# A fused attention and two-layer chain: q turned in 32x32 blocks, tokens in natural order, a new start list

## The chip, the cores and the metric

One NeuronCore of one Trainium2 chip runs the whole program. The metric is the time of one execution on the device in microseconds (us), the median of several runs; lower is better. The engines are TensorE (PE in the profile; PEld are its weight loads), VectorE (DVE), ScalarE (ACT), GpSimd (POOL) and SyncE (SP), whose queue issues most DMAs.

## The reference

Inputs: q, k, v of shape (8 batches, 8 heads, 576 tokens, 64), phi of shape (8, 8, 576, 32), and four weight matrices of doubles: 512x2048 and 2048x512 for each of two layers. Cut to what matters:

```python
a = softmax(phi, axis=2 (tokens))           # per batch, head and memory slot
k_m = einsum('bhsm,bhsd->bhmd', a, k)       # 32 memory slots a head
v_m = einsum('bhsm,bhsd->bhmd', a, v)
attn = softmax(q @ k_m^T / 8, axis=-1)      # over the 32 slots
x = (attn @ v_m) as (8*576 tokens, 512)     # heads side by side
x = square(relu(x @ w_in)) @ w_out          # first layer
h = x @ w2_in
out = (h - tanh(h)) @ w2_out                # second layer
```

## The kernel before, in words

The work has two layers in time. In the first, tokens go in 16 units of 288 (two for a batch); a unit takes 16 steps, one for each 128 of the 2048 hidden channels. In the second, tokens go in nine blocks of 512, again 16 steps each. Every large matmul is split into a high and a low part (hi*hi, hi*lo, lo*hi), so a step of the first layer is six matmuls into h (L425) and twelve into four accumulators (L454 to L456), all with 288 columns. The kernel doesn't form attn @ v_m: `u_make` multiplies v_m of a batch into 512 columns of w_in (u, L285), and h is u times the attention weights.

`att_a(b, g)` handles four heads (g = 0 or 1) of batch b. It loads phi, k and v with tokens in six chunks of 96, takes the maximum of phi over tokens (L216, a transpose on TensorE L221, a second maximum L223, a broadcast matmul L229), subtracts and exponentiates (L232, L236), sums over chunks on GpSimd (L239 to L241), multiplies with v and k (L246, 6 chunks x 4 heads; L248 for the sum), scales (L255), transposes (L261) and copies into `vt` and `kt`.

`att_b(b, o)` handles the four even or the four odd heads. It loads q in chunks of 96 tokens, transposes it on TensorE (L320, twelve a call) and copies it by ScalarE (L325, L326), multiplies with kt (scores, L334, eight matmuls of 64 rows by 32 columns), turns the scores in 32x32 blocks on VectorE (L343), makes the softmax with VectorE, GpSimd and ScalarE (L347 to L357), turns back (L360), and writes the hi (L364, ScalarE) and lo part (L366, GpSimd) of the attention weights. Tokens of a batch are dealt to the chunks in turn, p*6 + c, and the two units of a batch each hold tokens of all chunks by that order; a unit needs both calls of `att_b`.

The weights come as 64-bit doubles and are converted by `conv`: the absolute value on ScalarE (L144), then four VectorE instructions (L146 clamp, L148 shift and mask, L149 sign, L150 low bits). The 16 tiles of w_in go to `w1_conv`, the 16 of w_out to `wo_conv`, which splits them on GpSimd (L186). The second layer's 32 tiles are converted during the first layer and stored to DRAM (`w2_conv`).

The order of instructions is written by a manual schedule. Each piece of work is a generator; at each `yield` it names the buffers that it wants next, and it goes on only when they are free. For the first two batches and a part of the third, the text `ORDER` lists which generator is advanced next (i: att_a, j: att_b, w and o: conversions, u: u_make, S: a step of the first layer); what can't go on is tried again later. `step(s)` issues the h matmuls three steps ahead of the accumulating ones. The other batches start at fixed steps (`at_step`): for batch b, with s = 32(b-1) - 20, att_a at s and s + 8, att_b at s + 10 and s + 17. Engines run their instructions in order, so a waiting instruction holds up those behind it on its engine.

The output is stored by 70 DMAs on SyncE's queue and two on ScalarE's (L609), in pieces that follow the dealt order of tokens.

Of the kernel before, what the change touches and what calls it, by code (L numbers as in the profile page):

```python
# [9 lines left out]
F32 = mybir.dt.float32  # L10
# [11 lines left out]
P = 128  # L22
SP = 96
NC = 6
HT = 288
FT = DFF // P
# [14 lines left out]
w00 w00 o11 w02 i01 o0 w11 i00 u01 o2 w10 o8 w22 o12 j00 i00 i01 w02 w01 w02 i00 o0 i21 i00 i00 o3 j11 o0 w00 i00 w03  # L41
w20 w02 i00 w02 w00 o3 w10 i00 w01 w01 o0 w03 w03 w12 w10 i00 i01 j01 w02 j00 o1 o2 i00 o0 j00 i01 w00 w02 j01 j01 i20
w00 w13 i00 i00 i00 o12 w00 w03 o0 o4 w31 o1 i01 i10 i01 o4 w23 o0 j00 o9 j01 i01 w03 o1 j01 i01 j01 w01 w10 j01 o2
i01 w01 u00 o4 o15 i01 o2 i01 u01 o12 o2 i01 w03 w21 i01 i01 w03 o1 w01 j01 j01 o4 w13 o13 o0 j01 o4 o1 j20 w11 w00
u00 u00 j01 j01 w11 j01 o2 o4 w21 i00 o6 u00 o2 o12 w11 w21 o1 o3 w12 o4 o1 o4 j01 j00 j00 j01 o1 j00 w30 j00 w31 j00
w21 o12 o7 j01 i10 j01 i10 i10 o2 i10 w11 j00 i10 i11 o12 j01 o3 o2 j00 i10 o12 i10 w10 j11 w31 w31 i11 o0 w02 j00 o12
w12 i10 w03 i11 j00 j00 o5 o4 o5 o3 w13 o3 i10 j00 j00 o14 S i10 o10 i11 w12 i11 w13 o5 i10 j00 j11 S i11 w00 w12 i11
w01 S S o3 i11 w20 w11 o3 i11 i10 o5 i01 i20 j11 o10 o3 S i11 S j11 w13 w10 w11 o7 i10 o7 w13 o7 w32 w00 w32 o6 j11
w33 o8 i11 i11 o7 i11 u10 S u12 j11 j11 j11 o6 j10 S o7 o5 o7 o5 w10 j11 j11 o6 j10 w12 S u01 o5 j10 u01 o5 j11 w12
u10 i20 o7 u01 o10 o6 j10 o6 j10 o8 j11 S u11 o7 o6 u10 o10 j11 w23 j01 j11 w21 j21 o6 w23 o10 j10 o1 j10 u12 j11 j11  # L50
j10 S j10 j20 o2 w23 S o8 j10 o10 w23 o8 o12 j10 w21 j10 w01 j10 S o8 w22 j10 j10 w22 S S o11 w20 w22 w21 w23 j10 j10
S w21 j20 u11 S i20 w21 u11 o8 w22 w02 o11 S j20 S w20 S j20 w31 o11 o10 o1 o10 w22 w22 j20 o9 o14 o11 w11 S o11 w31
# [12 lines left out]
i20 w32 j21 j21 S j21 j20 w21 w33 S j21 S i20 j20 w11 i20 j21 j21 j21 j21
# [3 lines left out]
W_LO = 2.0 ** -15  # L69
W_HI = float.fromhex("0x1.dffffep+16")  # L70
# [3 lines left out]
def moe_chain_kernel(ctx: ExitStack, tc: tile.TileContext, q, k, v, phi, w1i, w1o, w2i, w2o, out):  # L74
    nc = tc.nc
    w1i, w1o, w2i, w2o = (w.bitcast(I32) for w in (w1i, w1o, w2i, w2o))
    out_v = out.rearrange("(b p c) e -> b c p e", b=B, c=NC)
# [7 lines left out]
    p_s9 = pool("small9", 1)  # L85
    pool("pad0", 1).tile([P, 8], F32, name="pad0")
# [17 lines left out]
    a_kv = pool("a_kv", 4, att)  # L104
# [3 lines left out]
    a_kt = pool("a_kt", 2, att)  # L108
    a_one = pool("a_one", 1, att)
# [23 lines left out]
    def conv(src, out, p=None, ahead=1):  # L133
# [14 lines left out]
        nc.vector.tensor_scalar(fi, fi, 3, 0x3FFFFFF8, op0=ALU.logical_shift_left, op1=ALU.bitwise_and)  # L148
        stt(fi, raw[:, :, 1], -0x40000000, fi, op0=ALU.bitwise_and, op1=ALU.bitwise_or)  # L149
# [9 lines left out]
    def w1_conv(fc, pr, p=None):  # L159
        if pr == 0:  # L160
            yield "w1"
            w1[0, fc] = slot(p_w, [P, 4, 512], f"w1_{fc}")
        while (0, fc) not in w1:
# [6 lines left out]
        done.add(("stored", fc, pr))  # L170

    def w1_load(b, fc):
        while not {("stored", fc, pr) for pr in range(4)} | {("u", 1, c) for c in range(FC)} <= done:
            yield
# [25 lines left out]
    def att_a(b, g, p_kv):  # L200
        yield "ph kv" if p_kv is a_kv else "ph"
        ph = slot(a_in, [SP, 4, NC, M], f"phi{b}_{g}")
        heads = slice(4 * g, 4 * g + 4)
        nc.sync.dma_start(ph, phi[b, heads].rearrange("h (p c) m -> p h c m", c=NC))
        yield "" if p_kv is a_kv else "wo wo wo wo"
        kv = []
        for h in range(4 * g, 4 * g + 4):
            t = slot(p_kv, [SP, 2, NC, D], f"kv{b}_{h}")
            for i, src in enumerate((v, k)):
                nc.sync.dma_start(t[:, i], src[b, h].rearrange("(p c) d -> p c d", c=NC))  # L210
            kv.append(t)
        for _ in range(4 if b > 2 else 1):
            yield
        yield "e f"
        m1 = slot(p_f, [SP, P], "m1")
        nc.vector.tensor_reduce(m1, ph.rearrange("p h c m -> p h m c"), axis=AX.X, op=ALU.max)  # L216
        yield "b"
        mx = p_s.tile([P, 1], F32, tag="mx", name="mx")
        den = p_s.tile([P, 1], F32, tag="den", name="den")
        t = psum(ps_b, "m1T")  # L220
        nc.tensor.transpose(t[:, :SP], m1, ident[:SP, :SP])  # L221
        yield "-"
        nc.vector.reduce_max(mx, t[:, :SP], axis=AX.X)  # L223
        dg = slot(p_f, [P, P], "dg")
        nc.scalar.activation(dg, ident, AF.Copy, scale=mx)
        give("b")
        yield "b"
        t = psum(ps_b, "mb")
        nc.tensor.matmul(t[:SP, :P], ones, dg)  # L229
        yield "-"  # L230
        e = slot(a_e, [SP, NC, 4, M], f"e{b}_{g}")
# [45 lines left out]
    def u_make(b, fc):  # L277
# [16 lines left out]
        if b:  # L294
            give("w1")
# [474 lines left out]
```

## Time and profile before

| what | value |
|---|---|
| median of 3 runs | 1581.09 us (1577.79 to 1581.84) |
| span of the profiled execution, first to last instruction | 1578.4 us |
| the median less that span | 2.7 us |
| busy share PE, PEld, DVE, ACT, POOL | 97%, 84%, 66%, 55%, 38% |
| data moved | 163 MB, 103 GB/s over the span |

The profile is of one execution, and durations are its own; the profiled execution's own time is the span and the small part around it, for which the table's third row stands. PE is busy when any matmul is under way; matmuls overlap, so the sum of their durations is more than PE's busy time, and prices of small matmuls are read from start times. The idle time of an engine that is not the bottleneck costs nothing.

### The profile page before, as it was taken

The page shows a single profiled execution, that of the slowest core. Times are in us where ns is not written, and L with a number is a line of the kernel's source. Part 1 is how long each engine was busy: PE and PEld are TensorE (multiplying, and loading weights), DVE is VectorE, ACT ScalarE, POOL GpSimd, SP SyncE. Part 2 cuts the span into 40 slices and gives each one's busy share as a digit, 9 for nine tenths or more (in the row PEclk, how much of TensorE's full clock was granted, in tenths as well). Part 3 has the DMA queues.
Part 4 walks back from the last instruction along what each step waited for, and adds up shares of the span by engine and source line. Part 5 has one row for each costly group of instructions (what it writes and reads, how often), then busy time and mean ns, then how long its engine had stood idle before and what let it go on. Part 6 is the DMA issues. An engine that isn't in the chain of part 4 may idle for free.

```text
span 1578.4 us, 26135 instructions
## 1 busy us (share of the span) xinstructions
PE 1523.9 (97%) x9904; PEld 1329.9 (84%) x9904; DVE 1043.0 (66%) x1436; ACT 868.1 (55%) x1849; POOL 605.2 (38%) x578
## 2 busy tenths in 40 slices
PE   4688999999999999999999999999999999999998
PEld 2577999999999999999988888888888888888887
DVE  5878444454535545430088888888889888888886
ACT  3576677666667676665554444444444444444433
POOL 2556465443534443443334232333324242333321
PEclk9999999999999999999999999999999999999999
DMA  9447566563745555431480101010010101010000
GB/s 329 152 139 175 185 154 171 175 213 111 239 138 196 181 174 173 137 123 69 150 308 1 42 12 43 11 31 24 1 41 14 42 13 43 12 44 11 25 3 27
DMA packets 89854, 163.06 MB, mean 103 GB/s; under 512 B 12416, under 2 KB 65664, under 8 KB 86656
## 3 DMA queue, kind: packets, MB, share of 16 engines
q1 hardware_dynamic: 86080, 157.52, 31.4%
q0 software_dynamic: 3456, 3.54, 1.7%
q8 instruction: 78, 1.28, 0.3%
q14 instruction: 48, 0.39, 0.1%
q10 hardware_dynamic: 192, 0.33, 0.1%
HBM read 117.96 MB, written 43.38 MB: 102 GB/s over the span
## 4 chain that ended last, share of the span: by engine, by line
PE 91%; DVE 3%; DMA 3%; ACT 2%; issue 1%; POOL 1%; SPq 0%; ACTq 0%; POOLq 0%
PE h L545 25%; PE h L425 13%; PE o L591 8%; PE o L590 8%; PE o L589 8%; PE acc L456 8%; PE acc L455 8%; PE acc L454 8%; PE u L285 2%; PE vkm L246 1%; PE qT L320 1%; DMA w_d<-w 1%; PE sc L334 1%; DVE wf L150 1%; DMA raw<-in_moe_w_in 1%
## 5 line engine op out<-in xcount | busy, mean ns | idle before, releaser
L545 PE MATMUL h<-x,wi 128*128 128x512 f32 x1728 | 414.7, 389 | 0.0
L575 POOL TENSOR_TENSOR gl<-pl,gh 128x512 fp32r<-128x512 f32 x144 | 187.9, 1305 | 535.7 <-PE o L590 517.2
L545 PEld LDWEIGHTS h<-x,wi 128*128 128x128 f32 x1728 | 324.2, 188 | 67.5 <-POOL x L525 0.2
L442 POOL TENSOR_TENSOR g<-gg,g 128x288 fp32r<-128x288 f32 x256 | 226.1, 902 | 366.2 <-ACT g L441 284.3
L557 ACT ACTIVATE u<-h 128x512 f32<-128x512 f32 x144 | 86.1, 598 | 418.3 <-PE h L545 418.3
L456 PE MATMUL acc<-g,wo 128*128 128x288 f32 x1024 | 301.8, 295 | 0.0
L454 PE MATMUL acc<-g,wo 128*128 128x288 f32 x1024 | 301.5, 294 | 0.2 <-ACT xs L465 0.2
L455 PE MATMUL acc<-g,wo 128*128 128x288 f32 x1024 | 301.3, 294 | 0.0
L425 PE MATMUL h<-aT,u 128*128 128x288 f32 x1536 | 259.3, 304 | 5.0 <-ACT gg L437 3.9
L425 PEld LDWEIGHTS h<-aT,u 128*128 128x128 f32 x1536 | 217.2, 190 | 39.3 <-issue 20.0
L589 PE MATMUL o<-wo,gh 128*128 128x512 f32 x576 | 224.1, 389 | 0.0
L590 PE MATMUL o<-wo,gh 128*128 128x512 f32 x576 | 224.1, 389 | 0.0
L591 PE MATMUL o<-wo,gl 128*128 128x512 f32 x576 | 224.1, 389 | 0.0
L454 PEld LDWEIGHTS acc<-g,wo 128*128 128x128 f32 x1024 | 192.8, 188 | 0.5 <-ACT xs L465 0.4
L455 PEld LDWEIGHTS acc<-g,wo 128*128 128x128 f32 x1024 | 192.6, 188 | 0.0
L456 PEld LDWEIGHTS acc<-g,wo 128*128 128x128 f32 x1024 | 192.6, 188 | 0.0
L560 DVE SCALAR_TENSOR_TENSOR pl<-u 128x512 f32<-128x512 f32 x144 | 99.5, 691 | 94.7 <-ACT u L557 94.7
L437 ACT ACTIVATE gg<-h 128x288 f32<-128x288 f32 x256 | 104.8, 409 | 88.8 <-PE h L425 86.3
L564 DVE SCALAR_TENSOR_TENSOR pl<-pl,u 128x512 f32<-128x512 f32 x144 | 148.6, 1032 | 0.0
L565 DVE COPY_PREDICATED pl<-m,th 128x512 f32<-128x512 int32 x144 | 140.2, 974 | 4.9
L590 PEld LDWEIGHTS o<-wo,gh 128*128 128x128 f32 x576 | 108.1, 188 | 22.6
L591 PEld LDWEIGHTS o<-wo,gl 128*128 128x128 f32 x576 | 108.1, 188 | 22.3
(86 smaller groups left out, 1977.2 us busy)
## 6 DMA issues: line engine op xcount, KB each, us to landing
w<-w_d SPq DMA_DIRECT2D x24, 1024.0 KB, 6.2
raw<-in_moe_w_in SPq DMA_DIRECT2D x32, 512.0 KB, 4.5
raw<-in_moe_w_out SPq DMA_DIRECT2D x32, 512.0 KB, 5.5
w_d<-w2s SPq DMA_DIRECT2D x32, 512.0 KB, 3.1
kv<-in_v SPq DMA_DIRECT2D x64, 144.0 KB, 4.6
kv<-in_k SPq DMA_DIRECT2D x64, 144.0 KB, 4.5
q<-in_q SPq DMA_DIRECT2D x16, 576.0 KB, 5.7
x_d<-xs SPq DMA_DIRECT2D x64, 144.0 KB, 2.5
```

The source lines that it names most:

```text
L425: nc.tensor.matmul(t[:, :HT], uu[:, w, o, c], at[u // 2][:, x, o, u % 2 * HT:u % 2 * HT + HT], start=(n == 0), stop=(n == 5))
L442: nc.gpsimd.tensor_tensor(gl, gg, gh.bitcast(F32), op=ALU.subtract)
L454: nc.tensor.matmul(o, wh[:, c], gh, start=(f == a), stop=False)
L455: nc.tensor.matmul(o, wh[:, c], gl, start=False, stop=False)
L456: nc.tensor.matmul(o, wl[:, c], gh, start=False, stop=(f == z - 1))
L545: nc.tensor.matmul(t, wi[f][:, w, c, :], x, start=(n == 0), stop=(n == 11))
L564: stt(pl, pl, A0, u, op0=ALU.add, op1=ALU.mult)
L565: nc.vector.copy_predicated(pl, m.bitcast(I32), th)
L575: nc.gpsimd.tensor_tensor(lo, pl, hi.bitcast(F32), op=ALU.subtract)
L589: nc.tensor.matmul(o, gh[:, c], wh, start=(f == 0), stop=False)
L590: nc.tensor.matmul(o, gh[:, c], wl, start=False, stop=False)
L591: nc.tensor.matmul(o, gl[:, c], wh, start=False, stop=(f == FT - 1))
```

## The change

- `att_b` now handles a half of the tokens (r = 0 or 1) with all eight heads, and a unit needs only its own half. q of a batch is loaded once. For batches 1 to 7 it comes as 32x32 blocks (four DMAs, 32 partitions each, runs of 32 numbers), and VectorE's block transpose makes qt; the transposes on TensorE and the copies by ScalarE stay only for batch 0.
- Heads are grouped by four (g) in `kt`, the scores and `u`; a table `POS` says in which 32 columns each head lies.
- Tokens are in natural order. `att_a` has chunks of 128 tokens, four full ones and one of 64 whose rest is filled (phi with -3e38, k and v with 0). From batch 2 on k and v carry a column of ones, so that the sums come from the same matmul. Batch 0's second group has buffers and PSUM banks of its own.
- `conv` scales by a power of two on ScalarE and has three VectorE instructions.
- Waits on other generators are written as functions, so that the list doesn't advance a generator that can't go on.
- `ORDER` is new (598 entries, before 779). The first S is entry 86, before 204.
- Two output blocks of 128 tokens are stored by one DMA.

```diff
-NC = 6
+NC = 5
+NR = S - P * (NC - 1)
+NEG = -3.0e38
+TB = HT // 32
+POS = (0, 2, 1, 3, 2, 0, 3, 1)
...
+i00 i01 j00 w02 j01 i01 w00 i00 i01 i01 i01 i01 i01 w01 w02 i01 i00 i00 i00 i00 o2 i01 i01 w02 i01 w00 i01 w00 w00
+j00 w01 i00 w13 w01 w03 w03 w03 o0 o7 u11 i00 i00 o1 i00 i01 o1 i00 i00 i00 i01 i01 j00 o2 o3 j00 w00 o0 j01 j01 j00
+i00 w10 w02 j01 w02 j01 j01 i00 w12 w10 o0 w10 w00 j00 u00 j00 j00 j00 w02 j00 u00 w01 w11 w00 w00 S j01 w11 w03 j00
...
-        nc.scalar.activation(f, raw.bitcast(F32)[:, :, 1], AF.Abs)
-        yield
-        nc.vector.tensor_scalar(f, f, W_HI, W_LO, op0=ALU.min, op1=ALU.max)
+        nc.scalar.activation(f, raw.bitcast(F32)[:, :, 1], AF.Copy, scale=W_SCALE)
+        yield
         fi = f.bitcast(I32)
...
+        for x, src in zip(kv, (v, k)):
+            if dense:
+                nc.sync.dma_start(x[:, :, :NC - 1], src[b, heads, :n0].rearrange("h (p c) d -> p h c d", p=P))
+            else:
+                for h in range(4):
+                    nc.sync.dma_start(x[:, h, :NC - 1, :D], src[b, 4 * g + h, :n0].rearrange("(p c) d -> p c d", p=P))
+        for x, src in zip(kv, (v, k)):
+            nc.sync.dma_start(x[:NR, :, NC - 1, :D], src[b, heads, n0:].rearrange("h p d -> p h d"))
...
-        for c in range(NC):
-            for h in range(4):
-                nc.tensor.matmul(vkm[32 * h:32 * h + 32, :2 * D], e[:, c, h], kv[h][:, :, c, :],
-                                 start=(c == 0), stop=(c == NC - 1))
-        nc.tensor.matmul(vkm[:, 2 * D:2 * D + 1], s1[:, 0], ones[:SP, :1])
+        wd = D if dense else D + 1
+        for i in range(2 if own else 1):
+            for c in range(NC):
+                for h in range(4):
+                    x = kv[i][:, h, c] if own else (kv_d if dense else kv_s)[:, :, h, c]
+                    o = vkm[32 * h:32 * h + 32, i * D:(i + 1) * D] if own else vkm[32 * h:32 * h + 32, :2 * wd]
+                    nc.tensor.matmul(o, e[:, c, h], x, start=(c == 0), stop=(c == NC - 1))
+        if dense:
+            nc.tensor.matmul(vkm[:, 2 * D:2 * D + 1], s1[:, 0], ones[:, :1])
...
         for i in range(4):
-            for o in range(2):
-                nc.tensor.matmul(t[o][32 * i:32 * i + 32], vt[b][half(o), i], w[half(o), i])
+            for h in (i, i + 4):
+                r, p0 = half(h % 2), 32 * POS[h]
+                nc.tensor.matmul(t[h // 4][p0:p0 + 32], vt[b][r, h // 2], w[r, h // 2])
...
+            qs[b] = slot(a_q, [P, 4, 2 * TB, 32], f"q{b}")
+            for g in range(2):
+                for dh in range(2):
+                    src = q[b, 4 * g:4 * g + 4, :, 32 * dh:32 * dh + 32]
+                    p0 = 64 * g + 32 * dh
+                    nc.sync.dma_start(qs[b][p0:p0 + 32], src.rearrange("i (t p) d -> p i t d", p=32))
+            for _ in range(4 if b > 2 else 1):
+                yield
+        yield lambda: b in qs
         yield "qt"
         qt = slot(a_qt, [P, 4, HT], "qt")
...
+        if b:
+            nc.vector.transpose(qt.rearrange("p i (t n) -> p i t n", n=32), qs[b][:, :, r * TB:(r + 1) * TB])
...
         for i in range(4):
-            for r in range(2):
-                nc.tensor.matmul(t[r][32 * i:32 * i + 32, :HT], kt[b][half(r), 2 * i + o], qt[half(r), i, :])
+            for g in range(2):
+                p0 = 32 * POS[4 * g + i]
+                nc.tensor.matmul(t[g][p0:p0 + 32, :HT], kt[b][half(g), i], qt[half(g), i, :])
...
-            if (u // 2, f // 4) not in us or not {("b", u // 2, o) for o in range(2)} <= done:
+            if (u // 2, f // 4) not in us or ("b", u // 2, u % 2) not in done:
                 return False
...
+                if i % 2:
+                    q_out = nc.scalar if last else nc.sync
+                    q_out.dma_start(out[c0 - P:c0 + P, :].rearrange("(t p) e -> p t e", p=P), acc["t"])
```

## Rows read from the trace of the kernel before

**Rows 1.** The page: busy time by engine, and PE in 40 slices.

```profile
PE 1523.9 (97%) x9904; PEld 1329.9 (84%) x9904; DVE 1043.0 (66%) x1436; ACT 868.1 (55%) x1849; POOL 605.2 (38%) x578
...
PE   4688999999999999999999999999999999999998
```

**Rows 2.** Busy time by stretch: PE, PEld, DVE, ACT, POOL; granted clock, DMA share, GB/s.

```profile
0.00:63.10 63.10, 26.93 (x237) 16.96 (x238) 45.14 (x74) 24.19 (x48) 21.94 (x26) 1.00 0.78 253
63.10:160.00 96.90, 85.00 (x689) 74.91 (x688) 76.36 (x105) 68.97 (x165) 53.98 (x53) 0.98 0.61 164
160.00:1573.10 1413.10, 1411.93 (x8982) 1237.98 (x8981) 920.96 (x1258) 774.61 (x1637) 529.23 (x500) 1.00 0.30 92
1573.10:1578.40 5.30, 0.00 (x0) 0.00 (x0) 0.57 (x2) 0.37 (x1) 0.00 (x0) 0.83 0.58 179
```

**Rows 3.** PE's timeline, start-up: start, duration, line, count, idle time before and releaser.

```profile
12.22 3.13 PE L246 MATMUL vkm<-kv,e 96*32 96x128 f32 x48 [4.59 <-ACT e L236]
...
29.05 3.09 PE L246 MATMUL vkm<-kv,e 96*32 96x128 f32 x48 [0.48 <-DMA w_d<-w]
...
63.89 3.01 PE L425 MATMUL h<-aT,u 128*128 128x288 f32 x11 [0.20 <-POOL aT L366]
```

**Rows 4.** PE's timeline in the first layer, same columns.

```profile
300.68 0.29 PE L456 MATMUL acc<-g,wo 128*128 128x288 f32 x1
300.81 0.66 PE L320 MATMUL qT<-ident,q 96*128 96x96 f32 x6
...
302.13 0.29 PE L454 MATMUL acc<-g,wo 128*128 128x288 f32 x1
...
303.58 0.29 PE L456 MATMUL acc<-g,wo 128*128 128x288 f32 x1
...
304.50 0.29 PE L454 MATMUL acc<-g,wo 128*128 128x288 f32 x1
...
313.31 0.71 PE L334 MATMUL sc<-qt,kt 64*32 64x288 f32 x16
...
328.54 1.09 PE L285 MATMUL u<-w,vt 64*32 64x512 f32 x16
...
336.90 0.29 PE L456 MATMUL acc<-g,wo 128*128 128x288 f32 x1
337.12 1.52 PE L246 MATMUL vkm<-kv,e 96*32 96x128 f32 x48
338.56 0.38 PE L248 MATMUL vkm<-ones,s 96*128 96x1 f32 x2
338.81 1.05 PE L425 MATMUL h<-aT,u 128*128 128x288 f32 x6
339.70 0.29 PE L454 MATMUL acc<-g,wo 128*128 128x288 f32 x1
```

**Rows 5.** DVE's groups by line, 5 to 160 us: busy us, mean ns, idle before.

```profile
L146 DVE TENSOR_SCALAR w<-w 128x512 f32<-128x512 f32 x14 | 12.0, 855 | 6.3 <-ACT w L144 5.5 <-DMA w_d<-w 0.7
...
L146 DVE TENSOR_SCALAR wf<-wf 128x512 f32<-128x512 f32 x15 | 7.2, 482 | 5.3 <-ACT wf L144 5.3
...
L360 DVE STREAM_TRANSPOSE aT<-sm 128x576 f32<-128x576 f32 x4 | 3.1, 775 | 2.2 <-POOL sm L357 2.2
```

**Rows 6.** Busy time in one batch of the first layer (32 steps).

```profile
400.00:489.80 89.80, 89.80 (x808) 83.69 (x808) 44.36 (x66) 61.43 (x145) 39.61 (x44) 1.00 0.56 179
```

**Rows 7.** POOL's timeline: lo part of the first att_b.

```profile
49.69 1.74 POOL L366 TENSOR_TENSOR aT<-aT,aT 128x576 fp32r<-128x576 f32 x1 [1.72 <-ACT aT L364]
```

**Rows 8.** A stretch with one 16 KB load; q's issues: KB, us to landing.

```profile
1188.00:1188.40 0.40, 0.40 (x3) 0.34 (x2) 0.36 (x2) 0.40 (x1) 0.00 (x0) 1.00 0.27 40
...
q<-in_q SPq DMA_DIRECT2D x16, 576.0 KB, 5.7
```

**Rows 9.** DMA issues over the whole span: KB, us to landing.

```profile
w_d<-w2s SPq DMA_DIRECT2D x32, 512.0 KB, 3.1
...
out<-osb ACTq DMA_DIRECT2D x1, 128.0 KB, 2.8
```

More of the change, by code (lines that the diff above doesn't have):

```diff
@@ L170, in w1_conv, with w1_user @@
         done.add(("stored", fc, pr))
+        w1_user(fc)
+    w1_users = collections.Counter()
+    def w1_user(fc):
+        w1_users[fc] += 1
+        if w1_users[fc] == 5:
+            give("w1")
     def w1_load(b, fc):
-        while not {("stored", fc, pr) for pr in range(4)} | {("u", 1, c) for c in range(FC)} <= done:
-            yield
+        yield lambda: {("stored", fc, pr) for pr in range(4)} | {("u", 1, c) for c in range(FC)} <= done
         yield "w1"
@@ L328, in att_b @@
[L328 to L331 removed]
+        if b:
+            nc.vector.transpose(qt.rearrange("p i (t n) -> p i t n", n=32), qs[b][:, :, r * TB:(r + 1) * TB])
+            q_used[b] += 1
+            if q_used[b] == 2:
+                give("q")
+        else:
+            for n in range(2):
+                yield "" if early else "b b"
+                t = [psum(ps_a if early else ps_b, f"qT{i}") for i in range(2)]
+                for i in range(2):
+                    for c in range(3):
+                        nc.tensor.transpose(t[i][:, c * SP:(c + 1) * SP],
+                                            qs[b][n][:, i, 3 * r + c].rearrange("p g d -> p (g d)"), ident[:SP, :SP])
+                q_used[b] += 1
+                if q_used[b] == 4:
+                    give("u", "u")
+                yield "-"
+                for i in range(2):
+                    nc.scalar.copy(qt[:, 2 * n + i], t[i][:, :HT])
+                if not early:
+                    give("b", "b")
@@ L363, in att_b, with ready @@
             at[b] = slot(p_at, [P, 2, 2, 2 * HT], f"aT{b}", F32R)
-        nc.scalar.copy(at[b][:, 0, o], a)
+        hi, lo = (at[b][:, x, :, r * HT:(r + 1) * HT] for x in range(2))
+        nc.scalar.copy(hi, a)
         yield
-        nc.gpsimd.tensor_tensor(at[b][:, 1, o], a, at[b][:, 0, o].bitcast(F32), op=ALU.subtract)
-        give("sm")
-        done.add(("b", b, o))
+        nc.gpsimd.tensor_tensor(lo, a, hi.bitcast(F32), op=ALU.subtract)
+        if (b, r) != (0, 1):
+            give("sm")
+        done.add(("b", b, r))
     active, wants = [], {}
     emptied = []
+    def ready(gen):
+        want = wants.get(gen, "")
+        if callable(want):
+            return want()
+        need = collections.Counter(want.strip("-").split())
+        if any(free[r] < n for r, n in need.items()):
+            return False
+        free.subtract(need)
+        return True
     def empty():
@@ L418, in l1_mm1 @@
         u, f, _, _ = seq[s]
-        assert {("b", u // 2, o) for o in range(2)} <= done, u
+        assert ("b", u // 2, u % 2) in done, u
         uu, c = us[u // 2, f // 4], slice(f % 4 * P, f % 4 * P + P)
```

273 lines of the change are left out of this document (141 added, 132 removed).

## The prediction

> **What bounds the kernel now.** I read the page's slices first [rows 1]: TensorE (PE) is at 90% or more in 35 of 40 slices; only the first four and the last lie lower. Busy time is 1523.9 of 1578.4 us, so nothing but TensorE work or the idle 54.5 us can change the time. The table by stretch [rows 2] places that idle time: 36.2 us lie ahead of 63.1 us, where the first matmul of the first layer stands; 11.9 lie between there and 160 us, 1.2 in the next 1413 us, 5.3 behind the last matmul.
>
> So there are two regimes. From 160 us on an engine other than PE costs nothing, and each TensorE instruction removed comes off the end whole. Ahead of 160 us the start-up sets the pace: loads, 32 weight conversions, the attention of two batches. There the rows of the first matmuls [rows 3] show what the first layer waits for: the second group of heads multiplies 16.8 us after the first (29.05 against 12.22), and the first h matmul runs free at 63.89, just released by the lo half of aT, GpSimd's last step of the *second* half of the attention. VectorE is busy 76.4 of the 96.9 us that follow [rows 2].
>
> The sum stands against the profiled span of 1578.4 us; the median of the runs is 1581.1, so 2.7 us lie around the span, and I keep them. As worked in the terms below: 1578.4 = 63.1 (first h) + 1496.9 (TensorE work behind it, 1510.0 less 13.1 idle) + 13.1 + 5.3.
>
> **The change, part by part.**
>
> *q turned by VectorE.* Batches 1 to 7 lose all their transposes on TensorE: 24 each, in four groups of six. From the last L456 ahead of such a group to the first L454 behind the h matmuls is 302.13 - 300.68 = 1.45 us; in a step with no guest it is 304.50 - 303.58 = 0.92 [rows 4]. So 0.53 us a group, 2.12 a batch. ScalarE loses eight copies of qT, which hide behind PE. VectorE gains two block transposes a batch of 128x1152; the trace has one of 128x576 at 775 ns [rows 5], so 1.55 us by proportion; two of the half size would be the same, and nothing in the trace makes it less than 0.78. In a batch of 89.8 us VectorE is 44.4 us busy [rows 6], so 3 us more are covered; without that cover it would be 3 us a batch.
>
> *Token chunks of 128.* Each group of heads multiplies 20 times instead of 24. A group now costs 339.70 - 336.90 - 0.92 = 1.88 us, of which the 48 instructions of L246 take 338.56 - 337.12 = 1.44 and the pair of L248 338.81 - 338.56 = 0.25 [rows 4]. Five chunks instead of six, 130 columns instead of 128, make 1.22: 0.22 saved. From batch 2 on the column of ones in kv takes over L248's sum, another 0.25. So 0.94 us a batch for batches 2 to 7 and 0.44 for batch 1. GpSimd's three additions a group go too, under cover.
>
> TensorE in all: 6 x (2.12 + 0.94) + 2.12 + 0.44 = 20.9 us. Wholly behind PE's bound for batches 2 to 7 (18.4); for batch 1, in the ramp, I count it too, since it stands in the work term and not in the idle one.
>
> *Token order, and what a unit waits for.* A unit of 288 tokens now needs one att_b, not both. Of the present chain that takes the wait from the second att_b's end back to the first's: GpSimd's L366 ends at 49.69 + 1.74 = 51.4 us [rows 7]. The new list also puts the loads of both head groups of batch 0 and of q ahead of the weights, and the second group has its own buffers and PSUM banks. What must land ahead of the first h is 4.1 MB of attention inputs and 2.1 MB of weights; at the 253 GB/s of the present start [rows 2] that takes 25 us, so the loads permit it. The two groups now lie 16.8 us apart; at best they follow each other at 3.1, which would give 13.7, at worst nothing is gained. I take half of the 16.8, as each chain also needs its turn on VectorE: first h at 51.4 - 8.4 = 43 us, bounds 38 and 51. Behind it then stand transposes and scores of the second half and the first group of batch 1, which ran ahead of it before: 1.06 + 0.71 (the scores' row) + 1.66 and three small ones like L248, 4.2 us [rows 4].
>
> *Three VectorE steps in a conversion.* L146 goes: 14 x 855 and 15 x 482 ns in the ramp, 19.2 us of VectorE [rows 5]; behind the ramp it is covered by PE. Against it stand the two transposes of batch 1 (3.1 us) and a first h that comes 20 us sooner, with some 15 us of VectorE's work still undone that was done before. The account is about even, so I keep the 13.1 us of idle time behind the first h; bounds 5 (VectorE keeps ahead) and 33 (the whole head start is given back).
>
> *Loads in short runs.* This is the part that could hurt. q of a batch becomes 9216 runs of 128 bytes (now 768 of 1536), k and v 9216 of 256 bytes, phi and the remainders some 1500. The nearest row: while the 128 runs of one 16 KB load of x2f go through, 0.40 us at a DMA share of 0.27 [rows 8]. At full share that is 0.11 us for 128 runs, 8 us for q; if a load can't go denser than it did there, 29 us. The present two q loads of 576 KB land in 5.7 us each [rows 8]. The engines idled three quarters of that stretch because 128 runs are only eight for each of sixteen engines, so I lean to the low end and take 13 us. The DVE transposes stand six steps behind the load, and the next thing behind them on VectorE's queue that TensorE waits for (the maximum of phi, for the second head group) three steps on; a step is 89.8 / 32 = 2.8 us, so q has 25 us. Cost: nothing, while it lands within that.
> The Trainium skill (DMA: Bandwidth & Descriptors, Specifications) states that a transfer needs 512 bytes for line rate and is done as read-modify-write below that; this speaks against the change. The row agrees so far as 40 GB/s at a share of 0.27 is 148 GB/s at full share, under the 253 of the start.
>
> *Stores and the tail.* Two output blocks go as one DMA of 512 KB, the last one too. A 512 KB store lands in 3.1 us, the last store now in 2.8 [rows 9]; I add 0.5 us. The other stores hide behind 16 steps.
>
> *Positions of heads.* Scores and u write the same eight 64x32 tiles in another order: no change, but see the third rival.
>
> **Sum.** 43.0 + (1496.9 - 20.9 + 4.2) + 13.1 + 5.3 + 0.5 = 1542.1 us of span; with 2.7 around it 1544.8, so 1545 us.
>
> **The rivals.**
> First: *the start gains nothing net.* Either the first h still stands near 63, or it comes sooner and the conversions give the 20 us back as idle time. For it: DMA at a share of 0.78 and VectorE at 79% in the ramp [rows 2]. Against: 19.2 us of VectorE's work is gone. Time: 1545 + 20 = 1565.
> Second, on the other side: *the short runs bind the DMA.* A batch has 37 us of other traffic (0.56 of 89.8 us is 50.3 [rows 6], less 4.1 MB at 179 / 0.56 = 320 GB/s). At 0.40 us for 128 runs the 20,000 new ones take 62 us: 100 us against a batch of 86.7, 13 us late in each of six batches, 1545 + 80 = 1625; VectorE waits for q, and the maximum of phi and TensorE behind it. It starts to cost at 0.32 us for 128 runs, and makes the kernel slower than before at 0.36. For it: the one stretch measured ran at 0.40. Against: engines idle there.
> The rule of the Trainium skill named above would be its cause.
> Third: *the new order of tiles lets the small matmuls overlap less.* Neighbours in u now share their rows where they shared their columns. If they ran half as dense, 32 calls of u would cost 1.1 us more each and 16 of the scores 0.7 [rows 4]: 1545 + 46 = 1591. Against: the 48 of L246 share all their rows and take 30 ns each [rows 4].
>
> **How the numbers follow.** Forecast 0.67 (own range 1531 to 1563: first h at 38 to 51, idle time 5 to some 24), first rival 0.19, second 0.10, third 0.04. What a measurement of this kernel can tell from no change is about 0.3%, 5 us: the first two cases are faster, 0.86; the second rival ends within 5 us of before in a small part of its band, 0.03; slower 0.11. The range takes in the forecast and nearly all of the first rival: 1529 to 1569.
>
> **What would show it.** Right: first L425 near 43 us; no qT behind the first batch; PE's idle time from 160 us to the last matmul still about 1 us; TensorE's busy time down by some 20 us plus what the slow early matmuls give. Wrong: waits of VectorE for q or of TensorE for kv (second rival); L285 groups of 16 longer than the 1.1 us they take now (third); a first L425 beyond 55 us, or PE waiting on conversions between 45 and 150 us for more than 30 us (first).

## The result, and the profile after

The changed kernel takes 1565.81 us (median of 4 runs, 1564.91 to 1567.44), the kernel before in the same rounds 1579.81 (1577.79 to 1581.84): a ratio of 0.9911, 95% interval 0.9897 to 0.9925. It is 14 us faster, where the forecast had 36. The time lies inside the range, near the first rival's 1565.

The page of the profile after, to stand beside [rows 1]: TensorE's busy time, its slices, and the granted clock in tenths.

```profile
PE 1508.3 (96%) x9624; PEld 1310.6 (84%) x9624; DVE 1001.4 (64%) x1386; ACT 850.1 (54%) x1793; POOL 582.8 (37%) x554
...
PE   4669899999999999999999999999999999999998
...
PEclk9979999999999999999999999999999999999999
```

TensorE is 15.6 us less busy, not 20.9 less, and the third clock digit is a 7, where the kernel before ran at full clock nearly throughout [rows 2]. The table by stretch places both (columns as in [rows 2]; the last row is the profile up to the first compressed product of batch 3).

```profile
0.00:45.20 45.20, 21.05 (x206) 12.18 (x206) 23.48 (x44) 17.30 (x36) 11.29 (x23) 1.00 0.82 258
45.20:160.00 114.80, 90.23 (x709) 78.11 (x710) 78.69 (x105) 72.08 (x163) 67.83 (x69) 0.88 0.72 179
160.00:200.00 40.00, 37.43 (x324) 30.46 (x323) 19.05 (x31) 24.90 (x60) 13.69 (x14) 0.91 0.47 148
200.00:1559.20 1359.20, 1359.20 (x8390) 1189.87 (x8388) 879.29 (x1207) 735.42 (x1535) 490.02 (x448) 1.00 0.31 91
1559.20:1564.60 5.40, 0.34 (x2) 0.00 (x0) 0.85 (x2) 0.44 (x2) 0.00 (x0) 0.74 0.50 194
...
0.00:281.00 281.00, 229.71 (x1917) 196.78 (x1918) 150.76 (x223) 173.68 (x398) 139.18 (x158) 0.94 0.72 189
```

And the row of the kernel before for that last stretch:

```profile
0.00:281.00 281.00, 231.80 (x2009) 202.79 (x2013) 175.44 (x256) 179.75 (x419) 146.32 (x159) 0.99 0.66 188
```

The two rows of 281 us are the whole story in little: TensorE stands idle 51.3 us of them after, 49.2 before. Idle time has only moved. The first h comes at 45.25 instead of 63.1, but behind it 114.80 - 90.23 + 40.00 - 37.43 = 27.1 us are idle, where the kernel before had 13.1; and a part of the work runs at the low level of the clock. Of the 27.1 us, 4.3 stand right behind the first h matmul and 12.3 between 95.99 and 119.31 us. From 200 us on TensorE never waits.

Where the idle time went shows in TensorE's timeline (start, duration, line, count, idle time before and its releaser). After, up to step 16 of the first layer:

```profile
11.14 1.30 PE L291 MATMUL vkm<-att,att 128*32 128x64 f32 x40 [1.47 <-ACT att L276]
...
17.82 2.36 PE L291 MATMUL vkm<-kv,e 128*32 128x128 f32 x40 [1.68 <-ACT e L276]
...
45.25 0.61 PE L516 MATMUL h<-aT,u 128*128 128x288 f32 x1 [4.29 <-ACT aT L446]
50.19 4.63 PE L516 MATMUL h<-aT,u 128*128 128x288 f32 x23 [4.33 <-POOL aT L448]
...
75.57 1.30 PE L291 MATMUL vkm<-kv,e 128*32 128x128 f32 x40
...
95.99 0.27 PE L260 MATMUL m1T<-ident,af 128*128 128x128 f32 x1
...
99.25 1.30 PE L291 MATMUL vkm<-kv,e 128*32 128x128 f32 x40 [1.68 <-ACT e L276]
103.96 0.59 PE L293 MATMUL vkm<-ones,af 128*128 128x1 f32 x2 [3.42 <-POOL af L282]
105.59 0.69 PE L308 MATMUL vkmT<-ident,af 128*128 128x128 f32 x2 [1.04 <-ACT af L300]
...
107.79 1.21 PE L411 MATMUL sc<-qt,kt 64*32 64x288 f32 x14 [0.42 <-ACT vt L317]
109.62 2.32 PE L333 MATMUL u<-w,vt 64*32 64x512 f32 x16 [0.61 <-DVE sm L423]
115.45 2.55 PE L333 MATMUL u<-w,vt 64*32 64x512 f32 x16 [3.51 <-DVE u L338]
...
119.31 1.09 PE L516 MATMUL h<-aT,u 128*128 128x288 f32 x3 [0.78 <-POOL aT L448]
```

The same products of batch 1 in the kernel before:

```profile
56.46 3.12 PE L246 MATMUL vkm<-kv,e 96*32 96x128 f32 x48 [1.92 <-ACT e L236]
...
73.31 1.52 PE L246 MATMUL vkm<-kv,e 96*32 96x128 f32 x48
```

Batch 0's two head groups now follow each other within 7 us ([rows 3]: 16.8). But batch 1's two come at 75.57 and 99.25 instead of 56.46 and 73.31, 26 us later for the second, though the first layer starts 18 us sooner. From 95.99 to 119.31 us TensorE has nothing in its queue but the links of that one chain: the maximum, the exponential, the product, the scaling, the scores, u, the softmax, each waiting for another engine.

In steady work the change does what was forecast. TensorE's timeline at the first products of two batches on end:

```profile
281.53 1.32 PE L291 MATMUL vkm<-kv,e 128*32 128x130 f32 x40
...
332.74 1.09 PE L333 MATMUL u<-w,vt 64*32 64x512 f32 x16
...
368.10 1.31 PE L291 MATMUL vkm<-kv,e 128*32 128x130 f32 x40
```

A batch takes 368.10 - 281.53 = 86.57 us, [rows 6] had 89.80: 3.23 saved, 3.06 forecast. u takes the 1.09 us that it took [rows 4]. The product at 281.53 stood at 280.85 us before:

```profile
280.85 1.52 PE L246 MATMUL vkm<-kv,e 96*32 96x128 f32 x48
```

So at batch 3 the changed kernel is 0.7 us *behind*; all of its gain, and a little more, comes after.

### The profile page after: what moved, and what is told of

Its sections match the earlier page's. It is cut to its first block, busy times and chain, and to the rows that moved or that the text cites. A ratio compares the mean times of both kernels' runs of the same rounds, so it can differ in the third digit from the quotient of the medians.

```text
span 1564.6 us, 25400 instructions
## 1 busy us (share of the span) xinstructions
PE 1508.3 (96%) x9624; PEld 1310.6 (84%) x9624; DVE 1001.4 (64%) x1386; ACT 850.1 (54%) x1793; POOL 582.8 (37%) x554
## 4 chain that ended last, share of the span: by engine, by line
PE 91%; DVE 2%; POOL 2%; ACT 2%; issue 1%; DMA 1%; SPq 0%; POOLq 0%; ACTq 0%; DVEq 0%
PE h L636 25%; PE h L516 13%; PE o L681 8%; PE o L680 8%; PE o L682 8%; PE acc L547 8%; PE acc L546 8%; PE acc L545 8%; PE u L333 2%; PE vkm L291 1%; PE sc L411 1%; DMA raw<-in_moe_w_in 1%; POOL wo L195 0%; POOL x_d L560 0%; DVE w L152 0%
## 5 line engine op out<-in xcount | busy, mean ns | idle before, releaser
L681 PEld LDWEIGHTS o<-wo,gh 128*128 128x128 f32 x576 | 108.2, 188 | 22.5
L680 PEld LDWEIGHTS o<-wo,gh 128*128 128x128 f32 x576 | 108.1, 188 | 22.5
```

The lines of the kernel that those rows point to most:

```text
L680: nc.tensor.matmul(o, gh[:, c], wh, start=(f == 0), stop=False)
L681: nc.tensor.matmul(o, gh[:, c], wl, start=False, stop=False)
```

## The experiments

All times are medians; the ratio is to the kernel before, run in the same rounds. The changed kernel's 1565.8 is the one to compare with.

| run | us (lowest to highest) | ratio [95%] | less 1565.8 |
|---|---|---|---|
| batch1_early | 1589.4 (1587.2 to 1591.7) | 1.0056 [1.0040, 1.0071] | +23.6 |
| batch1_early_steps_spread | 1589.9 (1586.6 to 1591.6) | 1.0055 [1.0041, 1.0070] | +24.1 |
| second_group_early | 1584.1 (1581.5 to 1586.3) | 1.0028 [1.0017, 1.0038] | +18.3 |
| chain_interleaved | 1574.4 (1572.1 to 1575.8) | 0.9967 [0.9955, 0.9980] | +8.5 |
| chain_interleaved_fillers | 1576.1 (1574.3 to 1578.4) | 0.9979 [0.9970, 0.9988] | +10.3 |
| old_list | 1657.4 (1656.7 to 1658.1) | 1.0486 [1.0463, 1.0509] | +91.6 |
| q_long_runs | 1566.0 (1564.6 to 1568.6) | 0.9909 [0.9892, 0.9925] | +0.2 |
| conv_four_steps | 1572.7 (1571.8 to 1574.7) | 0.9960 [0.9947, 0.9974] | +6.9 |
| conv_two_steps | 1557.5 (1555.8 to 1557.8) | 0.9858 [0.9845, 0.9872] | -8.3 |
| conv_one_step | 1552.7 (1552.1 to 1553.2) | 0.9830 [0.9816, 0.9843] | -13.1 |
| first_steps_late | 1565.6 (1564.3 to 1566.2) | 0.9911 [0.9897, 0.9924] | -0.2 |
| first_h_5us_late | 1567.0 (1566.5 to 1568.6) | 0.9920 [0.9907, 0.9934] | +1.2 |
| first_h_12us_late | 1574.3 (1572.4 to 1574.4) | 0.9961 [0.9948, 0.9973] | +8.5 |
| fillers | 1562.8 (1561.5 to 1565.7) | 0.9897 [0.9883, 0.9910] | -3.0 |
| fillers_more | 1569.2 (1567.7 to 1570.7) | 0.9933 [0.9919, 0.9946] | +3.4 |
| second_group_left_out | 1564.0 (1562.7 to 1565.0) | 0.9898 [0.9882, 0.9915] | -1.8 |
| raw_in_wo_slots | 1565.8 (1565.1 to 1566.6) | 0.9911 [0.9898, 0.9925] | 0.0 |
| raw_in_wo_slots_interleaved | 1574.3 (1572.2 to 1575.7) | 0.9962 [0.9949, 0.9976] | +8.5 |

**Batch 1 earlier in the list.** My first theory (A) was that the list simply brings batch 1 too late; the rival (B) that the conversions leave it no room. The new entries from the fifth line of ORDER on:

```diff
+w13 j00 j00 j01 o3 j01 j00 o4 o15 j00 j00 w03 o0 w13 w23 o5 u12 w13 w03 o2 o0 j01 o0 o0 w11 o0 w02 i10 i10 i10
+j00 i10 i10 o1 j01 o1 w10 w00 w01 u00 u00 u00 o1 w03 j01 o1 o3 w10 o2 o3 o2 w10 j00 o1 o3 i21 o7 u03 w13 o1
+j00 i10 i10 i10 j10 j10 S i10 S i10 i11 i11 S S i10 i11 i10 i10 u01 w21 o5 w10 w22 o8 u13 o2 o2 j20 w30 w32
...
```

> The changed kernel with only its start list edited: the entries of batch 1's compressed attention (i10, i11), of its token attention j10 and of its first-layer inputs (u10, u11) stand earlier, between the softmax of batch 0 and step 12; steps and conversions keep their order. Theory A (the list brings batch 1 so late that TensorE has only that one chain left before unit 2): the serial stretch 96 to 119 us disappears, idle time behind the first h falls from 27.2 us to about 13, the time comes to 1545 to 1556 us. Rival B (the conversions on DVE, ACT and POOL are what the start lacks): the same idle time turns up before other conversions (wo, w), 1563 to 1568 us. Rival C (the loads of short runs hold the start back): 1562 to 1568 us, since batch 1's loads land no sooner than the queue lets them.

> The same list, and the five steps 13 to 17, which stood behind all conversions o11 to o15, stand between these, one after each nine entries. Theory A: another 2 to 6 us faster than with batch 1 early alone (1541 to 1552 us), because TensorE gets unit 2 as soon as its input is there. Rival B: no faster, or slower by some us, as the conversions come later. Rival C: no difference.

Both lost 24 us, which neither theory had. TensorE's timeline of batch1_early shows two of the places (lines are one lower here and in the other lists):

```profile
54.90 0.80 PE L266 MATMUL mb<-af,ones 128*128 128x128 f32 x2 [10.16 <-ACT af L262]
...
147.13 1.81 PE L515 MATMUL h<-aT,u 128*128 128x288 f32 x6 [16.48 <-ACT gg L527]
```

Queues run in program order: batch 1's mb, now ahead of the first h in TensorE's queue, held it for 10 us, and later a whole step waited 16 us. A milder list touched nothing ahead of step 6, but put batch 1's second group and j10, u10, u11 ahead of the conversions o11 to o15:

```diff
+o8 i10 o6 o5 o9 j10 i11 i11 o12 o7 S S o11 w01 o8 i11 i11 o6 i10 o7 o6 j21 S i11 i11 i10 o6 S i11 i11
+o11 w31 o11 o6 S i11 i11 i11 o7 o11 o10 o10 o11 o7 o7 o9 o7 S i11 i11 S j10 j10 j10 j10 u10 u10 u10 j10 j10
...
```

> The changed kernel with its start list edited only behind step 5: the second head group of batch 1 (i11) takes its maximum as soon as its phi has landed (about 81 us instead of 90.9), each of its stages stands behind one first-layer step, and j10, u10 and u11 come ahead of the conversions o11 to o15; everything up to the first h stays as it was. Theory A (the chain of batch 1 is placed too late): the stretch 96 to 119 us, where TensorE does 13 us of work, closes by 6 to 12 us, time 1553 to 1560 us. Rival B (VectorE, ScalarE and GpSimd lack the time for the conversions in the start): the conversions put back now are missed later, 1563 to 1570 us.

It lost 18 us. The timelines of SP's queue (the second column is the time that the issues took, waits included) and of TensorE:

```profile
102.46 21.38 SPq L142 DMA_DIRECT2D raw<-in_moe_w_out  x3
```

```profile
145.50 1.22 PE L410 MATMUL sc<-qt,kt 64*32 64x288 f32 x16 [8.89 <-DVE qt L384]
```

The conversions put back held the raw buffers; SP, which issues all loads in order, stood for 21 us, and batch 2's loads behind it came late. TensorE's line is the scores of batch 1's second half, whose q had been loaded from 59.93 us on: their transpose on VectorE (143.99 us) stood behind a conversion for which VectorE had waited 8.30 us. So the third list moved the chain forward one stage at a time, and put no more conversions behind step 13 than had to be:

```diff
+o8 i10 o6 o5 o9 j10 i11 i11 o12 o7 S S o11 w01 o8 i11 i11 o6 i10 o7 o6 j21 S i11 i10 i11 o6 S i11 o11
+w31 o11 o6 S o7 j10 o11 o10 o10 o11 o7 o7 i11 o9 o7 S i11 S i11 i11 o11 i11 o11 i11 o9 o12 j10 o12 o10 j10
...
```

> The changed kernel with its list edited behind step 5: the stages of i11, then j10, u10 and u11 come forward one at a time between the conversions o7 to o13, which keep their order and nearly all their places ahead of step 13. Theory A: the gap at 96 to 119 us closes by 3 to 8 us, 1558 to 1563 us. Rival B: what the chain gains on its way the conversions lose, 1564 to 1572 us.

It lost 8.5 us: rival B's side. TensorE and VectorE now stopped each other, as their timelines show:

```profile
97.24 0.40 PE L546 MATMUL acc<-g,wo 128*128 128x288 f32 x1 [3.70 <-POOL wo L194]
```

```profile
101.84 0.16 DVE L296 TENSOR_SCALAR den<-vkm 128x1 f32<-128x1 f32 x1 [8.51 <-PE vkm L292]
```

TensorE waited 3.7 us for a weight from GpSimd ahead of batch 1's product, and VectorE 8.5 us for that product with the next conversions queued behind it. The step 16 came no sooner (119.11 us). With all three lists theory A in its simple form falls.

The old list in the new kernel, two runs:

> The changed kernel with the start list of the kernel before. The list names the same pieces of work, but the pieces now stop at other places, so the old list runs in another order: the first step comes behind most conversions. Theory A and B: the start loses several tens of us, 1590 to 1630 us; the steady part keeps its 3.2 us a batch. Should it come near 1566 us, the list has little to do with the start.

The first h came at 134 us and the time was 1657.4, above the expected band. The same entries mean other pieces of work, so this says only that the list and the kernel belong together.

**The loads in short runs.**

```diff
-                    nc.sync.dma_start(qs[b][p0:p0 + 32], src.rearrange("i (t p) d -> p i t d", p=32))
+                    nc.sync.dma_start(qs[b][p0:p0 + 32], q[b, 4 * g + 2 * dh:4 * g + 2 * dh + 2].rearrange(
+                        "i s d -> (i s d)").rearrange("(p i t d) -> p i t d", p=32, i=4, t=18))
```

> The changed kernel, with q of batches 1 to 7 read in long contiguous runs (so q's numbers lie in other places and the attention output is not the reference's); the instructions of all engines and the bytes stay. Theory A: the issue of a q load falls from 7.8 us to about 0.4 us of SP's queue, but the time stays within 3 us of 1566. Rival C: 8 to 14 us faster, 1552 to 1558 us.

No difference (+0.2), so rival C falls for q. The k and v of batch 2, in runs of 256 bytes, and phi kept their short runs; they weren't tested apart. SP's queue at batch 1's q, after and then in q_long_runs:

```profile
60.14 7.80 SPq L378 DMA_DIRECT2D q<-in_q  x4
```

```profile
59.33 2.21 SPq L378 DMA_DIRECT2D q<-in_q  x4
```

**How many VectorE steps a conversion has.**

conv_four_steps takes the code of the kernel before:

```diff
-        nc.scalar.activation(f, raw.bitcast(F32)[:, :, 1], AF.Copy, scale=W_SCALE)
+        nc.scalar.activation(f, raw.bitcast(F32)[:, :, 1], AF.Abs)
         yield
+        nc.vector.tensor_scalar(f, f, W_HI, W_LO, op0=ALU.min, op1=ALU.max)
...
```

conv_two_steps leaves out the second of these lines (L153), conv_one_step both:

```diff
-        stt(fi, raw[:, :, 1], -0x80000000, fi, op0=ALU.bitwise_and, op1=ALU.bitwise_or)
-        stt(fi, raw[:, :, 0], 29, fi, op0=ALU.logical_shift_right, op1=ALU.bitwise_or)
```

> The changed kernel with the conversion of the kernel before: ScalarE's absolute value and four VectorE steps in place of three; the list stays. Some 29 conversions in the start get 0.5 to 0.85 us longer, 15 to 20 us of VectorE. Rival B: this comes back nearly whole, 1578 to 1586 us. Theory A: VectorE is late only where the first h and batch 1's chain stand behind it, 1570 to 1577 us.

> The changed kernel with one more conversion step left out (the 3 low bits of each weight's fraction stay zero, which changes the output a little). Some 25 us of VectorE's work leave the start. Rival B: 10 to 20 us faster than the changed kernel, 1546 to 1556 us. Theory A: 2 to 6 us faster, 1560 to 1564 us, as the chain of batch 1 waits for loads, ScalarE and GpSimd in turn.

> The changed kernel with two of the three VectorE steps of a conversion left out (sign and low bits of the weights are lost, so the output is not the reference's); list and everything else stay. Two, three and four steps gave 1557.5, 1565.8 and 1572.7 us, 7 to 8 us a step of some 15 to 23 us of VectorE in the first 160 us. Rival B (conversions bind the start): again about 8 us, 1548 to 1552 us. Theory A': from here on the wait chain of batch 1 alone holds TensorE, 1555 to 1558 us.

1572.7, 1565.8, 1557.5, 1552.7: from four steps to one each step gives 6.9, 8.3 and 4.8 us. VectorE's groups of the changed kernel, 0 to 160 us (busy us, mean ns of one | idle before), say what a step is:

```profile
L153 DVE SCALAR_TENSOR_TENSOR wf<-raw,wf 128x512 int32<-128x512 int32 x16 | 15.6, 976 | 0.5
L152 DVE SCALAR_TENSOR_TENSOR wf<-raw,wf 128x512 int32<-128x512 int32 x16 | 13.5, 841 | 0.5
L152 DVE SCALAR_TENSOR_TENSOR w<-raw,w 128x512 int32<-128x512 int32 x11 | 10.5, 958 | 0.4
L153 DVE SCALAR_TENSOR_TENSOR w<-raw,w 128x512 int32<-128x512 int32 x10 | 9.5, 954 | 0.3
```

L153 is 25.1 us of VectorE and worth 8.3, L152 24.0 and worth 4.8; the step more of conv_four_steps has 13.4 us there (8.8 + 4.6) and is worth 6.9. So the conversions do hold the start, at a fifth to a half of their time (a part of it ahead of the first layer: with three, two and one steps the h matmuls run free at 50.19, 47.49 and 45.32 us): the fourth step came out in theory A's band, the other two nearer to B's.

**What the head start is worth.** The first attempt moved only list entries:

> The changed kernel with steps -3 to 0 of the first layer moved in the list from the place behind batch 0's first half to just ahead of step 1 (some 30 entries later), so the first h comes some 8 to 15 us later; nothing else moves. If the head start is worth nothing because the rest of the start sets the pace (rival B), the time stays within 3 us of 1566. If each us of the first h counts (the forecast's account), 1574 to 1581 us.

The first h stayed at 45.0 us, since it waits for aT and not for its place; the run says nothing about the question. So the first h was held back in TensorE itself, by repeating its first matmul 60 and 100 times:

```diff
         t = psum(ps_h, "h")
+        if s == 0:
+            for _ in range(60):
+                nc.tensor.matmul(t[:, :HT], uu[:, 0, 0, c], at[0][:, 0, 0, :HT])
```

> The changed kernel with the first matmul of the first h done 60 times more ahead of it (the same operands, the result overwritten by the first h): about 10 us of TensorE from 45.2 us on, of which 5 lie in the gap to 50.2 us that is idle anyway, so the first layer starts some 5 us later. If the head start counts us for us (the forecast's account): 1570 to 1572 us. If the conversions set the pace of the start (rival B), TensorE only waits less later on: 1564 to 1568 us.

> The same with 100 matmuls, about 17 us, so the first layer starts some 12 us later, near 62 us and the place it had in the kernel before. The forecast's account: 1576 to 1579 us. Rival B: 1564 to 1571 us, the 23 us gap of batch 1's chain takes most of it.

The h matmuls that ran free at 50.19 us ran at 54.35 and 60.61, 4.2 and 10.4 us later; the time grew by 1.2 (rival B's band) and 8.5 (between the two). A delay of 4.2 us costs next to nothing, the 6.2 us beyond it cost 7.3, about us for us. In the second run batch 1's chain had moved by as much:

```profile
60.61 2.53 PE L519 MATMUL h<-aT,u 128*128 128x288 f32 x18
...
116.41 0.69 PE L308 MATMUL vkmT<-ident,af 128*128 128x128 f32 x2 [1.04 <-ACT af L300]
```

vkmT stood at 105.59, so it is 10.8 us later with the same wait of 1.04: that chain starts behind step 12 in TensorE's own queue, so an earlier or later first layer carries the gap along and doesn't fill it.

**Filling the gaps.** 38 matmuls on the identity (the expectation's 35 is a miscount; fillers_more has 67, not 74), written where the next matmul writes anyway:

```diff
+    def fill(t, n):
+        for _ in range(n):
+            nc.tensor.matmul(t[:, :P], ident, ident)
...
+        if (b, g) == (1, 1):
+            fill(vkm[:, 256:], 10)
         if dense:
             nc.tensor.matmul(vkm[:, 2 * D:2 * D + 1], s1[:, 0], ones[:, :1])
```

> The changed kernel with 35 matmuls of 128 columns more, which stand ahead of the waiting matmuls of batch 1's second head group and of u10 and u11, write where these write next, and change no result. They occupy TensorE in 8 of the gaps between 96 and 117 us. If the low granted clock (0.50 to 0.55 from 100 to 120 us) is a cost of its own that follows from the gaps, it rises above 0.8 there and the time falls by 3 to 7 us, to 1559 to 1563 us. If the clock only goes with the waits, the time stays at 1566 or rises by up to 4 us.

> The kernel of fillers with 74 matmuls of 128 columns instead of 35: also ahead of j10's scores, of the h of step 16, and more of them ahead of u11, vkm and vkmT, where the clock was still at 0.50 from 110 to 115 us. If the clock is a cost of its own, another 1 to 3 us (1560 to 1562 us); if the fillers now stand in the way, 1563 to 1566 us.

> The same list with the 35 filling matmuls of fillers. If the clock's cost is separate: 2 to 4 us under chain_interleaved. If the chain now leaves no gaps: within 1 us of it or above.

The stretch 100 to 120 us (columns of [rows 2]) after, and in fillers:

```profile
100.00:120.00 20.00, 10.23 (x77) 3.24 (x69) 14.83 (x23) 9.54 (x19) 12.12 (x13) 0.52 0.70 167
```

```profile
100.00:120.00 20.00, 14.06 (x144) 9.53 (x150) 15.15 (x24) 8.48 (x16) 12.16 (x14) 0.83 0.75 175
```

The granted clock rose from 0.52, nearly all at the low level of 1.2 GHz, to 0.83, and the median fell by 3.0 us; the two ratios' intervals overlap, so this is likely, not certain. fillers_more raised it to 0.90 and was 3.4 us slower: 18 of its matmuls stood ahead of u11, but they need the PSUM bank for which u11 waits, so their 6.9 us came behind that wait and not into it. On chain_interleaved the fillers gave nothing.

**One suspect at a time away.** First the chain itself: batch 1's second group keeps its yields and its loads and loses its instructions, but for three copies from batch 0.

```diff
+        if (b, g) == (1, 1):
...
+            nc.scalar.copy(kt[b][half(g)], kt[0][half(g)])
+            for o in range(2):
+                nc.scalar.copy(vt[b][half(o), 2 * g:2 * g + 2], vt[0][half(o), 2 * g:2 * g + 2])
```

> The changed kernel without the computation of batch 1's second head group (i11): its loads stay, its maximum, exponential, 40 products and transposes go, and batch 1 takes the compressed keys and values of batch 0 for heads 4 to 7 (the output is not the reference's). The list and all conversions stay. TensorE loses some 2 us of work and the waits of 0.8, 1.7, 3.4 and 1.0 us that stand between 96 and 106 us, DVE and GpSimd lose 5 and 4 us. If the place of this chain is what cost the head start: 8 to 12 us faster, 1554 to 1558 us. If the conversions would hold TensorE at the same place anyway: 2 to 4 us faster, 1562 to 1564 us.

Only 1.8 us faster. TensorE's and ScalarE's timelines:

```profile
107.99 1.21 PE L434 MATMUL sc<-qt,kt 64*32 64x288 f32 x14 [11.06 <-ACT kt L269]
```

```profile
106.47 0.66 ACT L148 ACTIVATE wf<-raw 128x512 f32<-128x512 f32 x1 [3.77 <-DMA raw<-in_moe_w_out]
107.03 0.60 ACT L193 CAST wo<-wf 128x512 fp32r<-128x512 f32 x1
107.65 0.29 ACT L269 COPY kt<-kt 64x128 f32<-64x128 f32 x1
```

The scores start where they started, 107.99 for 107.79. With the chain gone they wait for a copy on ScalarE, which stands behind a conversion whose raw weights have just landed. So the last experiment took that wait away, with raw weights loaded into free wo slots, and the entries that load o12 and o13 moved behind steps 7 and 9:

```diff
-    gens.update((f"o{f}", wo_conv(f, p_wo if f < 8 else None)) for f in range(FT))
+    gens.update((f"o{f}", wo_conv(f, p_wo if f < 14 else None)) for f in range(FT))
```

> The changed kernel with the raw weights of o8 to o13 loaded into free wo slots, as those of o0 to o7 are, in place of the two raw buffers, and the two list entries that load o12 and o13 moved ahead by some 35 entries; all else stays. If the raw buffers pace the start: SP's wait of 11.7 us at 91 us and ScalarE's waits for raw weights at 100 to 106 us go, batch 1's scores come 3 to 8 us sooner, 1557 to 1563 us. If not: 1564 to 1567 us.

> The same with the list of chain_interleaved (1574.4 us with two raw buffers). If that list lost its 8.5 us to the raw buffers: 1554 to 1562 us. If it lost them to the order on VectorE and GpSimd: 1570 to 1575 us.

No difference, and the interleaved list is as slow as before. The wait for raw weights is gone from ScalarE, and kt is copied at the same time as in the run without the chain, because now the chain itself arrives there:

```profile
106.08 0.47 ACT L299 ACTIVATE af<-vkm,den 128x256 f32<-128x256 f32 x1 [2.10 <-DVE den L297]
106.46 0.68 ACT L147 ACTIVATE wf<-raw 128x512 f32<-128x512 f32 x1
107.02 0.62 ACT L192 CAST wo<-wf 128x512 fp32r<-128x512 f32 x1
107.65 0.26 ACT L314 COPY kt<-vkmT 64x128 f32<-64x128 f32 x1
```

Two paths end within a us of each other, batch 1's chain and the conversions on ScalarE. The chain's transposes (vkmT) end at 107.30 us here and the conversion's cast at 107.64; in the changed kernel the two ends are 106.28 and 107.03, and kt is copied at 107.04. Either one away leaves the other. Both away at once wasn't tried.

## Why the prediction was right in direction and wrong in size

**TensorE's work, right.** The transposes and the shorter products give 3.23 us a batch for the 3.06 of the sum. From batch 3's first product to the end the kernel takes 1564.6 - 281.53 = 1283.1 us, before it took 1578.4 - 280.85 = 1297.6: 14.5 saved, where the sum has 5 x 3.06 - 0.5 = 14.8.

**The first h, right only by its first matmul.** That came at 45.25 for 43.0, in its bounds. But the sum took its 43.0 from the end of GpSimd's lo part of aT, 51.4 less 8.4, and by that mark the h matmuls run free at 50.19: 1.2 us sooner, not 8.4. GpSimd's timeline:

```profile
46.87 1.46 POOL L195 TENSOR_TENSOR wo<-wf,wo 128x512 fp32r<-128x512 f32 x1 [2.47 <-ACT wo L193]
48.29 1.84 POOL L448 TENSOR_TENSOR aT<-sm,aT 128x576 fp32r<-128x576 f32 x1
```

ScalarE had the hi part ready at 45.20; the lo part (L448) stood behind the split of a converted weight, for which GpSimd itself had waited. These 4.3 us count below as idle time behind the first h.

**The step that failed** is "The account is about even, so I keep the 13.1 us of idle time behind the first h". It measured 27.1. The second term that was off is the work behind the first h, in which the sum had no price for a lower clock. With the work behind the first h 7.0 us longer than forecast (1487.2 for 1480.2), the first h 2.2 later and the tail 0.7 shorter, that is the whole miss: 14.0 + 7.0 + 2.2 - 0.7 = 22.5 us, the 1564.6 of the span less 1542.1. The start as a whole gained nothing (-0.7 us at batch 3), so the first rival was right in its price; of its cause, the conversions, the runs bear out a part.

What stood in its place:
- The account weighed VectorE's time alone. The end of the fourth conversion step was put at 19.2 us of VectorE and came out at 6.9 us of time (conv_four_steps); of the head start, which was counted whole, 4.2 us are worth next to nothing (first_h_5us_late).
- I charged the work that moved behind the first h as 4.2 us of TensorE. What moved with it was batch 1's chain of waits, 26 us later for its second group, and behind step 12 in TensorE's queue nothing else is left, so 12.3 us of idle time stand there. In the kernel before its links lay between other work. That the chain alone is the price isn't shown: without it the kernel is only 1.8 us faster, as the conversions hold the scores at the same place (second_group_left_out).
- The waits bring the clock down: 12 us of work between 105 and 123 us run at a granted clock of 0.50, which costs 6 us. Work at 60 to 63, 123 to 125 and 173 to 180 us runs low too. Added up in steps of half a us from the first h to 200 us (busy time times the missing share of the clock, an estimate), the low level costs 12.0 us after and 1.7 before. That is more than the 7.0 us by which the work came out too long; the rest of the work came out some 3 us shorter than the sum. That the clock can be had back apart from the waits is likely (fillers, 3 us).
- 8.5 us (the head start, by first_h_12us_late) and 6.9 us (the conversion step) ought to have come out of the start and didn't. I put that down to the list's other placements, by the sum and by the timelines; no run shows it by itself, no list that I tried gives them back, and each lost more. Whether another order, or both paths to the scores near 107 us made shorter at once, would close the gap stays open.

**The other rivals, out.** *Short runs bind the DMA*: from 300 to 600 us the DMA share rose, and TensorE waited for nothing. The rows of before and after:

```profile
300.00:600.00 300.00, 300.00 (x2671) 280.03 (x2670) 147.80 (x224) 205.35 (x480) 132.36 (x148) 1.00 0.57 182
```

```profile
300.00:600.00 300.00, 300.00 (x2640) 280.07 (x2639) 143.99 (x222) 204.69 (x474) 126.70 (x135) 1.00 0.68 190
```

At the old 182 / 0.57 = 319 GB/s the new 190 would be a share of 0.595, so the short runs take 0.085 x 300 = 25 us in 3.5 batches, 7 a batch (an estimate; q_long_runs, with 193 GB/s at a share of 0.64, has some 11 of the 25 left), where the rival's price of 0.40 us for 128 runs made 62. In the row behind that price [rows 8] the engines idled three quarters of the time. A batch's q, four loads issued within 6.6 us and landing 5.3 us behind, takes about 12 us, for the 13 that I took. The Trainium skill (DMA: Bandwidth & Descriptors, Specifications) has transfers under 512 bytes fall short of line rate. By that rule the trace agrees in kind, 279 GB/s at full share for 319, but the loss stays under TensorE's bound. *Tiles overlap less*: u kept its 1.09 us. The block transposes cost VectorE 1.37 us each for the estimated 1.55, all under cover.

## What to carry to other kernels

When a change lets the first tile start sooner, ask what the same engines no longer do ahead of it: here a start bought by putting the next tile's chain of dependent steps back came out even, and what stood against it was idle time and a lower clock, not the moved work. The measure is one row for both kernels, idle time up to the same late landmark, instead of the time of the first matmul. Where removing a suspect changes nothing, look at what the waiting instruction waits for now: two paths that end together hide each other.

## What the runs showed of the hardware

SP is busy with a load longer the more runs it has: four q loads of 2304 runs of 128 bytes take it 7.80 us, the same bytes in long runs 2.21, and four loads of k of 512 runs of 256 bytes 2.60 (at 146.34 us). It cost nothing here, as SP had the time.

GpSimd and VectorE take longer side by side. GpSimd's timeline of the changed kernel, and VectorE's in the same moments:

```profile
98.71 3.01 POOL L195 TENSOR_TENSOR wo<-wf,wo 128x512 fp32r<-128x512 f32 x1
```

```profile
98.98 1.64 DVE L152 SCALAR_TENSOR_TENSOR wf<-raw,wf 128x512 int32<-128x512 int32 x1
100.65 1.63 DVE L153 SCALAR_TENSOR_TENSOR wf<-raw,wf 128x512 int32<-128x512 int32 x1
```

Elsewhere GpSimd's instruction takes 1.3 us (its median) and VectorE's 0.69, so a conversion step seems the dearer the more GpSimd has to do beside it: of the changed kernel's 128 instructions of L152 and L153, all 23 that took 1.2 us or more overlap GpSimd's by at least 0.7 us. The Trainium skill (SBUF — State Buffer, Who interferes with whom) says that a VectorE instruction with two inputs in SBUF and a GpSimd instruction that reads SBUF block each other by an exclusive lock. These rows agree with it; no run here took it apart.
